# The third list of a routed expert layer goes through DRAM, with the low parts of one round's W2 on GpSimd and new urgencies for the searches

## The chip, the cores and the metric

One core of a Trainium2 chip runs the whole program. The metric is the device time of one execution in microseconds. Three executions of the kernel before took 650.06, 651.45 and 654.1 us, median 651.45. TensorE is the matrix engine (PE in the profile), VectorE is DVE, ScalarE is ACT, GpSimd is POOL; SyncE (SP) issues most transfers.

## The reference

```python
# q, k, v: 8 batches x 8 heads x 576 tokens x 64; heads 0-3: plain window of 32,
# heads 4-7: every 4th of the last 128 keys
attn = softmax(where(mask, q @ k.T / 8, -1e9)) @ v
x = attn, tokens as rows                         # 4608 x 512
logits = x @ w_gate                              # 8 experts
for idx in argsort(-logits.flatten()):           # best pair of token and expert first
    tok, e = idx // 8, idx % 8
    if assigned[tok] >= 0 or counts[e] >= 576: continue
    assigned[tok] = e; counts[e] += 1
out[assigned == e] = relu(x[assigned == e] @ w1[e]) @ w2[e]   # w1: 512 x 1024, w2: 1024 x 512
```

Each expert takes exactly 576 tokens. Inputs and result are float32.

## The kernel before

The first part computes the attention and the logits and writes the token rows to a DRAM tile `xd`; it ends near 200 us. The change does not touch it. The second part, `moe`, runs eight rounds, numbered 0 to 7 here. Round r serves the expert that fills up as the r-th, and its tokens are the r-th list (round 0 has the first list, round 2 the third).

A list is found by a search (`search`): eight steps, each a count on TensorE (`R.counts`, nine small matmuls, L841) and a chain of some ten small VectorE instructions (`R.step`, `R.remain`), one waiting for the other. Then `settle` finds the members, ranks them (L1118), closes the expert (`close`, `leave`, `start`: what the next search needs, and a copy of the choices on ScalarE, L982) and writes the list: `listing` makes flags on VectorE (`within`, L1176), a product on GpSimd and one on ScalarE, sums them on TensorE (`place`, L1195), and VectorE writes the indices (L1207).

`gather` fetches the 576 rows of x by five indirect transfers on GpSimd (four of 128 rows, one of 64). For the first rounds TensorE transposes each tile (L1396, four transposes into the one PSUM tile `ptx`). From round `QUARTERS` on it calls `spread` instead: the gathered tile goes to DRAM (L1420) and comes back in four pieces (L1424), arranged so that VectorE's transpose of 32x32 blocks (L1430) gives what is wanted, with the contraction rows in another order; W1 for these rounds comes from `in_moe_w1q`, which has the same order. Only two row tiles (`XG[5]`, `XG[6]`) serve the five gathers of `spread`; a gather waits until the store of the tile before the last is done.

Everything is multiplied in two parts: a high part rounded by ScalarE (`xh`, `w1h`, `w2h`, `hb`) and a low part, the difference (`xl`, `w1l`, `w2l`). The first product (L1460) takes, for each block of 128 hidden units, columns 0 to 255 of the list (its first two tiles) and columns 256 to 575 (the other three); the second (L1506 to L1511) takes one tile of tokens after the other. The low parts of the weights are VectorE subtractions (L1245), except those named in `ADDED`: there ScalarE writes the negated high part (L1271) and a GpSimd transfer adds the raw weight to it (L1273).

The order of the instructions on each engine is fixed when the program is built, by a list scheduler (`Schedule.run`). Each operation has a cost, dependences, perhaps an added latency `lat`, and a boost. Its due time is the end of the plan less the longest path behind it (its own cost included) less its boost. Of the operations that are ready on an engine the one due first is taken; others may fill a gap. Boosts are in nanoseconds: a larger one makes an operation more urgent. `B_C[r]` is the boost of the chain of search r and of closing its list, `B_L` that of the list itself, `B_G` that of gathers. On the chip every engine then works through its own order, waiting at each instruction for what it needs; a transfer waits in the same way on the queue of the engine that issues it.

Of the kernel before, what the change touches and what calls it, by code (L numbers as in the profile page):

```python
# [37 lines left out]
HI16, LO16 = -4128832, 4128831  # L38
HIGH = 65536.0
TOL_DVE, TOL_ACT, TOL_POOL, TOL_PE, T_W = 100, -50, 200, 500, 730  # L40
T_P, T_S, AHEAD = 310, 2200, 5
B_L, B_G, B_T, B_X, B_H, B_HL, B_Y, B_S, B_W = 23000, 27000, 15000, 0, 20000, 17000, 28000, -15000, 1500
RAW1, D_R, NQ, AHEAD_W = 8, 262, (2, 2), (3, 4)
QUARTERS, POOLED, T_B, T_H, B_R = 3, range(0), 5000, 2500, 20000
ADDED, T_A, T_G, T_L = (("2", 0), ("1", 1), ("2", 1)), 4500, 4500, 3500
T_D = {"1": 5000, "2": 4000}
NS, B_E, DIRECT, T_I = (2, 2), 3000, 7, 5000
B_C = (0, 2500, *(20000 + -16000 * (r >= QUARTERS) for r in range(2, 8)))
P_U, B_A, B_K, B_V, B_P, TOL_A, TOL_B, TOL_C, TOL_D = 4680, 15400, -5200, 14500, -105500, 650, 650, 300, 800
Q_ENG = (("POOL", "POOL", "POOL", "ACT"), ("DVE", "DVE", "ACT", "ACT"))  # L50
MSZ = (128, 128, 128, 128, 64)
# [119 lines left out]
class Schedule:  # L171
# [9 lines left out]
    def op(self, eng, cost, fn, deps=(), boost=0, lat=0, dma=0, buf=None, mode=64, tail=None):  # L181
        x = Op(len(self.ops), eng, cost, fn, deps, boost, lat, dma, buf)
        x.mode = mode
        x.tail = self.LAT if tail is None else tail
        for d in x.deps:
            d.users.append(x)
        self.ops.append(x)
        return x
# [1023 lines left out]
def moe(tc, ctx, C, R, xd, ROWS, w1, w1q, w2, out):  # L1212
# [8 lines left out]
    op = K.op  # L1221
# [24 lines left out]
    E, gemm1_end, x_users, got, gate = {}, {}, {}, {}, {}  # L1246

    def weights(n, r, f, deps):

        raw, old, use = RAW[n].take()  # L1250
        if n == "1" and r < len(AHEAD_W) and f == AHEAD_W[r]:

            gate[r] = op("POOL", 100, lambda: nc.gpsimd.memset(raw[:1, :1], 0.0), [got[r, 1], *old], B_G)
        if r in gate:
            deps = [*deps, gate[r]]

        def load():
            if n == "1":
                src = (w1 if r < QUARTERS else w1q)[bass.ds(E[r], 1), f].rearrange("o p d f -> p (o d f)")
            else:  # L1260
                src = w2[bass.ds(E[r], 1), f * 128:f * 128 + 128, :].rearrange("o p d -> p (o d)")
            nc.sync.dma_start(raw, src)

        ld = op("SP", 60, load, [*deps, *old], dma=T_W, lat=T_D[n] if r > 1 else T_L if n == "1" and r in gate and r else 0)
        h, oldh, useh = WH[n].take()
        l, oldl, usel = WL[n].take()
        first = n == "1" and r == 0
        hi = op("ACT", 525, lambda: act(h, raw), [ld, *oldh, st["rows"] if first else None], B_W)
        if (n, r) in ADDED:
            use.append(hi)  # L1270
            ne = op("ACT", 525, lambda: nc.scalar.activation(l, h.bitcast(F32), AF.Copy, scale=-1.0), [hi, *oldl], B_W)  # L1271
            useh.append(ne)
            lo = op("POOL", 1040, lambda: nc.gpsimd.dma_start(l, raw, accum_op=OP.add), [ne], B_W, lat=T_A)  # L1273
            use.append(lo)
        elif n == "2" and r >= 2 and f in POOLED:
            lo = op("POOL", 1350, lambda: sub(nc.gpsimd, l, raw, h), [ld, hi, *oldl], B_W)
            use += [hi, lo]
        else:
            lo = op("DVE", 600, lambda: sub(nc.vector, l, raw, h), [ld, hi, *oldl, st["list"] if first else None], B_W)
            use += [hi, lo]  # L1280
        useh.append(lo)
        return h, l, hi, lo, useh, usel


    def chain(eng, cost, fn, deps, boost=None):
        return op(eng, cost, fn, deps, B_C[len(scan)] if boost is None else boost)

    st, scan = {"place": None}, []

    def search(r):  # L1290
        scan.append(r)
        prev = st["next"]
        hold = gemm1_end.get(r - AHEAD) if r != 2 else gemm0[1]
        g = prev + [hold]
        for v in range(2):
            for it in range(4):
                early = 20000 if r == 1 and 4 * v + it < 1 else None
                p = chain("PE", T_P, R.counts, g if it == 0 else g[:1], early)

                def dve(v=v, it=it):  # L1300
                    R.step(it, v)
                    if it < 3:
                        R.remain(it, v)
                    if it == 3 and v == 0:
                        R.low(R.R, R.delta)
                        R.flags(R.V2, None, R.kstep(0, True))

                cost = T_S + (130, -330, -90, -1010 if v else 105)[it]
                g = [chain("DVE", cost, dve, [p, *g[1:]], early)]

        def which():
            R.count()
            R.fills()
            R.expert(R.largest())
            R.above()

        return chain("DVE", 2310, which, [g[0], st["fetch"]])

    def settle(r, e):

        if r == 0:
            m = rk = None
            nd = st["need"] = chain("DVE", 160, R.need_first, [], B_L)
        elif r < NE - 1:
            m = chain("DVE", 920, R.members, [e], B_L)
            rk = chain("PE", 70, R.ranks, [m], B_L)
            nd = st["need"] = chain("DVE", 270, R.need_of, [m, st.get("slots")], B_L)
        else:
            nd = chain("DVE", 400, R.rest, [e, st["left"], st["slots"]], B_L)
            rk = chain("PE", 70, R.ranks, [nd], B_L)  # L1330
        ac = chain("DVE", 1045, R.accept, [rk, nd], B_L)
        sl = st["slots"] = chain("DVE", 250, R.slots, [ac, st.get("digits")], B_L)
        ix, box = listing(r, sl)
        st["left"] = None
        if r == NE - 2:
            st["left"] = chain("DVE", 350, R.taken, [ac])
        elif r < NE - 1:
            cl = chain("DVE", 1930, R.close, [nd, ix if r == 0 else None])
            lv = chain("DVE", 830, R.leave, [cl, ac])
            gf = chain("DVE", 670, R.start, [cl])  # L1340
            st["next"] = [lv, gf]
        return ix, box

    def listing(r, sl):
        d = st["digits"] = op("DVE", 485, R.digits, [sl, st["place"]], B_L)
        t, old, use = PTR.take()
        lows, c1 = [], 0
        for n in OB[r > 0]:
            c0, c1 = c1, c1 + n
            lows.append((op("DVE", 110 + (36 if r == 0 else 26) * n, lambda c0=c0, c1=c1: R.within(c0, c1), [d], B_L), c0, c1))  # L1350
        halves = [(0, 14), (14, NCH)] if r == 0 else [(0, NCH)]
        xs = [(op("POOL", 150 + (30 if r == 0 else 18) * (c1 - c0), lambda c0=c0, c1=c1: R.by_chunk(c0, c1), [d], B_L),
               op("ACT", 250 + 9 * (c1 - c0), lambda c0=c0, c1=c1: R.by_row(c0, c1), [d], B_L)) for c0, c1 in halves]
        st["rows"] = xs[-1][1]
        prev = [*xs[0], *old]
        if r == 0:
            for (x, c0, c1), y in zip(lows, (xs[0], xs[1], xs[1])):
                prev = [op("PE", 27 * (c1 - c0), lambda c0=c0, c1=c1: R.place(t, c0, c1), [*prev, x, *y], B_L)]
        else:
            prev = [op("PE", 470, lambda: R.place(t, 0, NCH), [*prev, *(x[0] for x in lows)], B_L)]  # L1360
        st["place"] = prev[0]
        box = []
        ix = st["list"] = op("DVE", 780, lambda: box.append(R.indices(t)), prev, B_L)
        use.append(ix)
        return ix, box
# [71 lines left out]
    last, turns, gemm0, puts = [None], [], {}, {}  # L1437
# [110 lines left out]
    def round_(r):  # L1548
        e = None
        if r:  # L1550
            e = search(r) if r < NE - 1 else chain("DVE", 980, R.last, [st["fetch"], st["need"], st["left"]])
        en = st["fetch"] = EN[r] = op("SP", 100, lambda: fetch(r, R.eidx), [e])
        ix, BOX[r] = settle(r, e)
        X[r] = gather(r, ix, BOX[r])
        if r < NE - 2:
            lv, gf = st["next"]
            oc = (chain("ACT", 1055, lambda: R.copies(R.oh, nc.scalar), [lv]) if r else
                  chain("DVE", 640, lambda: R.copies(R.oh, nc.vector), [lv]))
            st["next"] = [oc, gf]
        W[r] = [weights("1", r, f, [en]) for f in range(NF)]  # L1560

    round_(0)
    for r in range(NE):
        W2 = [weights("2", r, f, [EN[r], X[r][-1][0] if r == 1 else None]) for f in range(NF)]
        expert(r, X[r], BOX[r], W[r], W2)
        if r + 1 < NE:
            round_(r + 1)
# [79 lines left out]
```

## Time and profile before

| | |
|---|---|
| median of three runs | 651.45 us (650.06 to 654.1) |
| profiled execution | 653.12 us, its span 651.4 us |
| TensorE busy | 618.2 us, 95% of the span |
| VectorE, ScalarE, GpSimd busy | 463.3, 304.4, 212.0 us |
| granted TensorE clock, mean | 0.975 |
| DMA | 110.97 MB, mean 170 GB/s |

The span is the time from the first to the last instruction; the rest of the profiled execution lies around it. Times in the rows below count from the span's start. Round 0's first product begins at about 206 us, round 1's at 264, round 2's at 325.5, and the rounds after it are 51 to 55 us long.

### The profile page before, as it was taken

To read this page: it belongs to the slowest core of one execution; us is meant where nothing else is said; L and a number is where in the kernel's file an instruction comes from. 1 tells how busy PE (TensorE), PEld (TensorE's weight loads), DVE (VectorE), ACT (ScalarE), POOL (GpSimd) and SP (SyncE) were. 2 spreads that over 40 slices of the span, in tenths; PEclk is the share of its full clock that TensorE was granted. 3 is DMA by queue.
4 is the path that set the end of the run, shared out by engine and by line. 5 is a ranking of instruction groups with operands and counts; after the bars stand their busy time and mean duration, and the time that the engine had idled before them with its cause. 6 is when DMAs were issued, how large, how long until landed. Compare 5 with 4: busy or idle time off the path is not lost.

```text
span 651.4 us, 18440 instructions
## 1 busy us (share of the span) xinstructions
PE 618.2 (95%) x7084; PEld 538.6 (83%) x7084; DVE 463.3 (71%) x1566; ACT 304.4 (47%) x675; POOL 212.0 (33%) x316
## 2 busy tenths in 40 slices
PE   7899899999858999999999999999999999999996
PEld 5788788879645988997799789789879979988985
DVE  4667577777678884799899999889889765624300
ACT  5676566666303825754445155235325425524211
POOL 6356467566004317333221221213112142011011
PEclk9899899999957999999999999999999999999999
DMA  8888898887206837997258338417716977302001
GB/s 240 228 245 238 236 261 253 218 244 203 80 3 191 222 82 195 284 189 253 76 157 273 107 109 268 156 62 254 212 41 211 272 229 234 107 34 73 1 25 48
DMA packets 68008, 110.97 MB, mean 170 GB/s; under 512 B 9168, under 2 KB 30544, under 8 KB 67920
## 3 DMA queue, kind: packets, MB, share of 16 engines
q1 hardware_dynamic: 58576, 84.62, 43.4%
q0 software_dynamic: 9344, 25.17, 14.5%
q8 instruction: 55, 0.90, 0.6%
q14 instruction: 33, 0.27, 0.1%
HBM read 78.69 MB, written 24.77 MB: 159 GB/s over the span
## 4 chain that ended last, share of the span: by engine, by line
PE 79%; DVE 8%; issue 5%; ACT 3%; DMA 2%; POOL 2%; SPq 0%; POOLq 0%; DVEq 0%; ACTq 0%
PE ph L1460 28%; PE py L1506 23%; PE px L550 4%; PE pS L538 4%; PE px L609 3%; PE py L1509 2%; PE py L1511 2%; PE pz L841 2%; PE pm L526 1%; PE pS L533 1%; PE pm L522 1%; PE pz L927 1%; DMA const<-in_cf 1%; POOL xg L1382 1%; PE ptx L1195 1%
## 5 line engine op out<-in xcount | busy, mean ns | idle before, releaser
L1506 PE MATMUL py<-w2h,hb 128*128 128x512 f32 x512 | 168.5, 396 | 0.0
L1460 PE MATMUL ph<-xh,w1h 128*128 128x256 f32 (+1 forms) x512 | 137.6, 299 | 0.8 <-ACT xh L1244 0.7
L1460 PE MATMUL ph<-xh,w1l 128*128 128x256 f32 (+1 forms) x512 | 136.2, 297 | 0.0
L1460 PE MATMUL ph<-xl,w1h 128*128 128x256 f32 (+1 forms) x512 | 136.2, 296 | 0.0
L1506 PEld LDWEIGHTS py<-w2h,hb 128*128 128x128 f32 x512 | 96.2, 188 | 18.9
L1244 ACT ACTIVATE hb<-ph 128x320 fp32r<-128x320 f32 (+2 forms) x192 | 59.8, 346 | 92.2 <-PE ph L1460 88.8
L1506 PE MATMUL py<-w2l,hb 128*128 128x512 f32 x256 | 99.8, 390 | 0.0
L1460 PEld LDWEIGHTS ph<-xh,w1h 128*128 128x128 f32 x512 | 91.9, 190 | 1.8 <-ACT xh L1244 0.9
L1460 PEld LDWEIGHTS ph<-xh,w1l 128*128 128x128 f32 x512 | 91.7, 190 | 0.1
L1460 PEld LDWEIGHTS ph<-xl,w1h 128*128 128x128 f32 x512 | 91.6, 190 | 0.0
L1532 POOL DMA_INDIRECT out<-y,idx x40 | 40.8, 1020 | 152.9 <-ACT y L1244 119.2
L1481 DVE SCALAR_TENSOR_TENSOR hb<-ph,hb 128x320 fp32r<-128x320 f32 (+1 forms) x128 | 57.0, 454 | 32.3 <-ACT hb L1244 29.5
L1244 ACT ACTIVATE y<-py 128x512 f32<-128x512 f32 (+1 forms) x40 | 23.9, 598 | 102.6 <-PE py L1506 91.3
L1414 POOL DMA_INDIRECT xg<-xd,idx x25 | 29.1, 1162 | 98.3 <-DMA rows<-xg 81.1
L492 ACT ACTIVATE E<-pS 128x384 f32<-128x384 f32 x96 | 44.9, 492 | 28.0 <-PE pS L538 27.3
L1506 PEld LDWEIGHTS py<-w2l,hb 128*128 128x128 f32 x256 | 48.2, 188 | 8.4
L550 PE MATMUL px<-v,E 128*64 128x65 f32 x1152 | 48.7, 224 | 5.0 <-issue 3.8
L538 PE MATMUL pS<-q,k 128*64 128x64 f32 x1152 | 53.0, 229 | 0.0
L550 PEld LDWEIGHTS px<-v,E 128*64 128x64 f32 x1152 | 42.4, 137 | 9.7 <-issue 5.8
L318 POOL COPY v<-v 32x520 f32<-32x520 f32 (+2 forms) x56 | 34.1, 633 | 49.1 <-DMA v<-in_vp 20.5
L538 PEld LDWEIGHTS pS<-q,k 128*64 128x64 f32 x1152 | 48.7, 144 | 0.0
L1245 DVE TENSOR_TENSOR w2l<-raw,w2h 128x512 fp32r<-128x512 f32 x48 | 31.7, 684 | 23.2 <-ACT w2h L1244 22.9
(217 smaller groups left out, 1123.6 us busy)
## 6 DMA issues: line engine op xcount, KB each, us to landing
raw<-in_moe_w SPq DMA_DIRECT2D x88, 256.0 KB
raw<-in_moe_w1q SPq DMA_DIRECT2D x40, 256.0 KB
rows<-xg SPq DMA_DIRECT2D x20, 256.0 KB
xg<-rows SPq DMA_DIRECT2D x80, 64.0 KB
qs<-in_qp SPq DMA_DIRECT2D x16, 288.0 KB
k<-in_kp SPq DMA_DIRECT2D x16, 288.0 KB
qs<-in_qd SPq DMA_DIRECT2D x16, 288.0 KB
k<-in_kd SPq DMA_DIRECT2D x16, 288.0 KB
```

Of the source, the lines that this page charges most:

```text
L318: f(t[:32, c0 + 1:c1 + 1], t[96:, c0:c1])
L492: e = self.op("ACT", 475, lambda j=j, pS=pS: nc.scalar.activation(self.E[:, 3 * j:3 * j + 3].rearrange("p c x -> p (c x)"), pS.tile[:, :38 ...
L538: x = nc.tensor.matmul(pS[64 * h:64 * h + 64, k, :, h], self.K[:, 32 * g:32 * g + 64], self.Q[:, g], start=False, stop=True, skip_group_ch ...
L550: x = nc.tensor.matmul(px[64 * h:64 * h + 64, c - c0, a], self.E[:, k, 64 * a:64 * a + 64], self.V[:, k, 2 * self.ui + a], start=True, sto ...
L609: x = nc.tensor.transpose(pt.tile[:, 128 * (c - c0):128 * (c - c0) + 128], xs[:, c, 2 * ui:2 * ui + 2].rearrange("p a d -> p (a d)"), C["i ...
L1244: act = lambda o, i, f=AF.Copy: nc.scalar.activation(o, i, f)
L1245: sub = lambda e, o, a, b: e.tensor_tensor(o, a, b, op=OP.subtract)
L1414: nc.gpsimd.indirect_dma_start(out=rows[:n], out_offset=None, in_=xd, in_offset=bass.IndirectOffsetOnAxis(ap=box[0][:n, m:m + 1], axis=0))
L1460: nc.tensor.matmul(o, a[:, d * 128:d * 128 + 128], b[:, d, c0:c1], start=((d, i) == pairs[0]), stop=((d, i) == pairs[-1]))
L1481: hl = op("DVE", 335 if j == 0 else 400, lambda: nc.vector.scalar_tensor_tensor(hb[:, CAP + c0:CAP + c1], o, 0.0, hb[:, c0:c1], op0=OP.max ...
L1506: nc.tensor.matmul(py, x, w, start=(f + i == 0), stop=(f == NF - 1 and i == 2))
L1532: s = nc.gpsimd.indirect_dma_start(out=out, out_offset=bass.IndirectOffsetOnAxis(ap=box[0][:n, m:m + 1], axis=0), in_=y[:n], in_offset=None)
```

## The change

- `QUARTERS` goes from 3 to 2: round 2's gather uses `spread`, and its W1 comes from `in_moe_w1q`.
- W2 of round 1 leaves `ADDED`: its eight low parts become GpSimd subtractions.
- In the planner, loads of round 1 get the latency of later rounds (W2 4000 ns, the first tiles of W1 5000 ns, instead of 0).
- The third list's search is no longer held until round 1's first product has begun.
- Boosts of the searches: the second list's falls from 2500 to -4000, the third's from 20000 to 10000, the fourth's rises from 4000 to 20000, those of the fifth to seventh from 4000 to 12000. The third list's flags (`within`) get 11000 instead of 23000. The cost of a count in the planner falls from 310 to 280 ns.

```diff
-T_P, T_S, AHEAD = 310, 2200, 5
-B_L, B_G, ... = 23000, 27000, ...
+T_P, T_S, AHEAD = 280, 2200, 5
+B_O, B_L, B_G, ... = 11000, 23000, 27000, ...
-QUARTERS, POOLED, T_B, T_H, B_R = 3, range(0), 5000, 2500, 20000
-ADDED, T_A, T_G, T_L = (("2", 0), ("1", 1), ("2", 1)), 4500, 4500, 3500
+QUARTERS, T_B, T_H, B_R = 2, 5000, 2500, 20000
+ADDED, T_A, T_G, T_L = (("2", 0), ("1", 1)), 4500, 4500, 3500
-B_C = (0, 2500, *(20000 + -16000 * (r >= QUARTERS) for r in range(2, 8)))
+B_C = (0, -4000, 10000, 20000, 12000, 12000, 12000, 4000)
...
-  ld = op("SP", ..., lat=T_D[n] if r > 1 else T_L if n == "1" and r in gate and r else 0)
+  ld = op("SP", ..., lat=T_D[n] if r > 1 else T_L if n == "1" and r in gate and r else T_D[n] if r else 0)
...
-        elif n == "2" and r >= 2 and f in POOLED:
+        elif (n, r) == ("2", 1):
             lo = op("POOL", 1350, lambda: sub(nc.gpsimd, l, raw, h), [ld, hi, *oldl], B_W)
...
-        hold = gemm1_end.get(r - AHEAD) if r != 2 else gemm0[1]
+        hold = gemm1_end.get(r - AHEAD)
...
-            lows.append((op("DVE", ..., lambda: R.within(c0, c1), [d], B_L), c0, c1))
+            lows.append((op("DVE", ..., lambda: R.within(c0, c1), [d], B_O if r == 2 else B_L), c0, c1))
```

## Rows read from the trace of the kernel before

**Rows 1.** Busy time by stretch: stretch, length, engines' busy us (instructions), PEclk, DMA share, GB/s.
```profile
265.40:325.70 60.30, 59.76 (x478) 52.03 (x478) 54.50 (x235) 33.86 (x73) 22.27 (x28) 1.00 0.70 188
325.70:380.60 54.90, 54.90 (x398) 48.23 (x396) 49.76 (x171) 22.38 (x51) 12.50 (x17) 1.00 0.51 164
...
250.90:264.60 13.70, 13.70 (x72) 10.97 (x70) 2.80 (x5) 5.20 (x9) 9.04 (x13) 1.00 0.85 238
264.60:293.50 28.90, 28.77 (x268) 28.01 (x267) 25.76 (x117) 19.92 (x47) 11.48 (x14) 1.00 0.96 222
```
**Rows 2.** All waits of TensorE, 211.3 to 646 us: total us, times, longest.
```profile
PE ptx L1396 <- DVE xl L1245: 0.2, 1, 0.2
PE pz L841 <- issue: 0.2, 1, 0.2
```
**Rows 3.** TensorE's timeline: start us, duration, line, operands, count.
```profile
313.01 0.60 PE L1396 MATMUL ptx<-const,xg 128*128 128x128 f32 x4
...
313.68 0.40 PE L1506 MATMUL py<-w2l,hb 128*128 128x512 f32 x1
313.92 0.63 PE L1506 MATMUL py<-w2h,hb 128*128 128x512 f32 x2
...
325.51 0.63 PE L1460 MATMUL ph<-xh,w1h 128*128 128x256 f32 x4
...
328.51 0.75 PE L1460 MATMUL ph<-xh,w1h 128*128 128x320 f32 x4
```
**Rows 4.** VectorE's groups over the span: count, busy us, mean ns, idle before.
```profile
L1481 DVE SCALAR_TENSOR_TENSOR hb<-ph,hb 128x320 fp32r<-128x320 f32 (+1 forms) x128 | 57.0, 454 | 32.3 <-ACT hb L1244 29.5 <-issue 1.3
...
L1430 DVE STREAM_TRANSPOSE xg<-xg 128x512 f32<-128x512 f32 (+1 forms) x25 | 15.9, 647 | 3.2 <-DMA xg<-rows 3.2
```
**Rows 5.** Low parts of W2, 262 to 300 us: ns min/median/max, first and last start.
```profile
L1273 POOL DMA_DIRECT2D w2l<-raw x8: 853/862/919, 271.5 to 285.9; - x8
```
**Rows 6.** GpSimd's timeline.
```profile
244.56 0.84 POOL L1181 TENSOR_TENSOR rx<-oa,const 128x360 bf16<-128x360 bf16 x1 [0.91 <-DVE oa L1176]
...
412.39 0.91 POOL L1414 DMA_INDIRECT xg<-xd,idx  x1 [10.13 <-DMA rows<-xg]
```
**Rows 7.** VectorE's timeline.
```profile
244.39 2.30 DVE L1176 TENSOR_TENSOR ob<-si,const 128x384 bf16<-128x384 int16 x6
...
248.94 0.33 DVE L1207 SCALAR_TENSOR_TENSOR idx<-t 64x5 int32<-64x5 f32 x2
...
298.11 1.79 DVE L1176 TENSOR_TENSOR ob<-si,const 128x384 bf16<-128x384 int16 x6
...
302.73 0.33 DVE L1207 SCALAR_TENSOR_TENSOR idx<-t 64x5 int32<-64x5 f32 x2
...
388.12 0.33 DVE L1207 SCALAR_TENSOR_TENSOR idx<-t 64x5 int32<-64x5 f32 x2
...
431.96 0.42 DVE L1245 TENSOR_TENSOR xl<-xg,xh 128x256 fp32r<-128x256 f32 x1
```
**Rows 8.** TensorE's timeline, counts, ranks and a first product.
```profile
206.31 0.44 PE L841 MATMUL pz<-G,ohr 128*128 128x64 bf16 x9
...
217.79 0.44 PE L841 MATMUL pz<-G,ohr 128*128 128x64 bf16 x9
...
242.19 0.21 PE L1118 MATMUL pz<-ge,const 128*128 128x72 bf16 x1
...
264.60 0.44 PE L841 MATMUL pz<-G,ohr 128*128 128x64 bf16 x9
...
268.13 0.82 PE L1460 MATMUL ph<-xh,w1h 128*128 128x320 f32 x4
...
291.28 0.21 PE L1118 MATMUL pz<-ge,const 128*128 128x72 bf16 x1
```
**Rows 9.** ScalarE's timeline.
```profile
250.30 1.16 ACT L982 ACTIVATE ohr<-oh 128x1152 bf16<-128x1152 bf16 x1 [0.74 <-DVE oh L960]
...
265.77 0.38 ACT L1244 ACTIVATE xh<-ptx 128x256 fp32r<-128x256 f32 x1
```

More of the change, by code (lines that the diff above doesn't have):

```diff
@@ L40 @@
 TOL_DVE, TOL_ACT, TOL_POOL, TOL_PE, T_W = 100, -50, 200, 500, 730
-T_P, T_S, AHEAD = 310, 2200, 5
-B_L, B_G, B_T, B_X, B_H, B_HL, B_Y, B_S, B_W = 23000, 27000, 15000, 0, 20000, 17000, 28000, -15000, 1500
+T_P, T_S, AHEAD = 280, 2200, 5
+B_O, B_L, B_G, B_T, B_X, B_H, B_HL, B_Y, B_S, B_W = 11000, 23000, 27000, 15000, 0, 20000, 17000, 28000, -15000, 1500
 RAW1, D_R, NQ, AHEAD_W = 8, 262, (2, 2), (3, 4)
-QUARTERS, POOLED, T_B, T_H, B_R = 3, range(0), 5000, 2500, 20000
-ADDED, T_A, T_G, T_L = (("2", 0), ("1", 1), ("2", 1)), 4500, 4500, 3500
+QUARTERS, T_B, T_H, B_R = 2, 5000, 2500, 20000
+ADDED, T_A, T_G, T_L = (("2", 0), ("1", 1)), 4500, 4500, 3500
 T_D = {"1": 5000, "2": 4000}
 NS, B_E, DIRECT, T_I = (2, 2), 3000, 7, 5000
-B_C = (0, 2500, *(20000 + -16000 * (r >= QUARTERS) for r in range(2, 8)))
+B_C = (0, -4000, 10000, 20000, 12000, 12000, 12000, 4000)
 P_U, B_A, B_K, B_V, B_P, TOL_A, TOL_B, TOL_C, TOL_D = 4680, 15400, -5200, 14500, -105500, 650, 650, 300, 800
@@ L1262, in load @@
             nc.sync.dma_start(raw, src)
-        ld = op("SP", 60, load, [*deps, *old], dma=T_W, lat=T_D[n] if r > 1 else T_L if n == "1" and r in gate and r else 0)
+        ld = op("SP", 60, load, [*deps, *old], dma=T_W, lat=T_D[n] if r > 1 else T_L if n == "1" and r in gate and r else T_D[n] if r else 0)
         h, oldh, useh = WH[n].take()
@@ L1349, in listing @@
             c0, c1 = c1, c1 + n
-            lows.append((op("DVE", 110 + (36 if r == 0 else 26) * n, lambda c0=c0, c1=c1: R.within(c0, c1), [d], B_L), c0, c1))
+            lows.append((op("DVE", 110 + (36 if r == 0 else 26) * n, lambda c0=c0, c1=c1: R.within(c0, c1), [d], B_O if r == 2 else B_L), c0, c1))
         halves = [(0, 14), (14, NCH)] if r == 0 else [(0, NCH)]
```

## The prediction, made before the result was known

> **What bounds the kernel now.** I read the page first, then the stretches of the expert part, then TensorE's waits, then the timelines of TensorE, VectorE and GpSimd around the third list. [...] Between 211.3 and 646 us it waits twice, 0.2 us each [rows 2]. So a microsecond of TensorE work taken out of rounds 0 to 2 is a microsecond of time, as long as the next operands are there. No other engine is at its bound for a whole round, but VectorE is close: 54.50 of 60.3 us in round 1, against 2.80 of 13.7 us just before the search for the third list [rows 1].
>
> **What the change takes from TensorE.** Five groups of transposes for the third list (four of 128 rows, one of 64) leave round 1's second product. One group starts at 313.01 and the second product behind it at 313.68; two neighbouring products without a group are 0.24 us apart (313.68 and the one behind it, 313.92), so a group costs 0.67 - 0.24 = 0.43 us [rows 3]. Five make 2.2 us, and with them goes the 0.22 us for which one group waited for the single PSUM tile [rows 2, 3]: 2.4 us. The upper bound is five whole durations of 0.60 us and the wait, 3.2 us; the lower, with the small group at half price and the wait staying, 2.0 us. I take 2.4, since it is measured in place.
>
> **What it adds.** VectorE gets the five transposes in blocks that each of the five later lists has, 25 in 15.9 us, so 3.2 us [rows 4]; its subtractions stay. They are hidden: the 13.7 us ahead of the search held 2.80 us of VectorE work [rows 1], and the search moves there. If that room were not used, VectorE would be at 57.7 of some 58 us in round 1 and the low parts of the hidden rows would come late, up to 3.2 us on TensorE. The five stores and twenty reads of the scratch trip go through SyncE, behind and before the weight loads; the trip's reads wait there for its store. Round 2 carries the same trip for the fourth list, with the same loads queued behind it, at 54.90 us of TensorE in 54.9, so I cost the queue at nothing [rows 1]; without that cover a load of W1 for round 2 would be late, by a wait of some us at 323. DMA had a share of 0.96 from 264.6 to 293.5 us [rows 1]: eight accumulating transfers of 256 KB leave just this stretch, and the trip (1.1 MB out, 1.1 MB back) falls mostly in the next.
>
> **W2 of round 1.** Eight ScalarE negations and eight GpSimd transfers (0.86 us to issue each, the last at 285.9 us) go [rows 5]; eight GpSimd subtractions of 128x512 f32 come. No such row exists. The nearest is a two-input GpSimd product, 128x360 bf16, at 0.84 us [rows 6]: by elements 1.2 us, twice that if the wider type counts in full. I take 1.2 us, by the same kind of operation. Eight are 10 us (up to 19), where GpSimd had 11.48 us busy of 28.9 [rows 1], seven of them in the transfers that go. The last high part and its negation were done when the last transfer was issued, at 285.9 us [rows 5], so the last low part is there near 287 to 288; the second product starts at 293.5. Cover about 5 us; if it goes, TensorE waits on the last low parts, and the list's gathers queue behind them on GpSimd. The later counting of weights (4 and 5 us in the planner instead of 0) only moves their loads ahead and their uses back; cost nothing, with the same cover.
>
> GpSimd's arithmetic also costs VectorE something. Six flag products of VectorE took 2.30 us with the GpSimd product lying on them and 1.79 us when it was nearly over: 0.51 us for 0.84 us [rows 6, 7]. Eight subtractions then cost VectorE 0.6 x 10 = 6 us if all lie on such operations, 0 if none does; I take a third, 2 us, as an estimate: most of a search step is small operations with one input. [...]
>
> **Is the third list in time?** This decides. Before, its indices are ready at 303.06 us and round 2's first product begins at 325.51, its second column block at 328.51 [rows 3, 7]. With 2.4 us less these become 323.1 and 326.1; the last low part of x is wanted 1.2 us later, at 327.3. A trip through the scratch, measured for the fifth list: indices at 388.45, the fifth tile's low part done at 432.38: 43.9 us, because only two row tiles serve five gathers (the fifth runs at 412.39, after 10.13 us of waiting for a store) [rows 6, 7]. So the indices are wanted by 327.3 - 43.9 = 283.4 us, 19.7 us sooner than before. What gives this, each an estimate from rows:
> - The hold goes: its first count ran at 264.60, just behind round 1's first product [rows 8]; its inputs are ready at about 251.5, when ScalarE has copied the choices [rows 9]. 13.1 us.
> - From ranks to indices the third list took 11.8 us (291.28 to 303.06), since closing the list and starting the next search came between; the second list took 7.1 (242.19 to 249.27) [rows 7, 8]. With the scratch path ahead of it, the list is now due sooner than the next search, even with its boost cut to 11000. 4.7 us.
> - In the empty 13.7 us a search step meets no low part of hidden rows, 0.45 us each [rows 4]. Four or so of the eight steps lie there: 1.7 us.
> - The second list's search loses 6500 of boost, but the planner counts backwards: by its own costs the two-tile trip lengthens the path from that search by some 13 us more than the old path through round 1, so it is due about 6 us sooner in all. Its second step ran 11.5 us after its first (206.31, 217.79) [rows 8], so there is room. 0 to 6 us.
> Sum 19.5 to 25.5, less 2 for GpSimd: 17.5 to 23.5, against 19.7. I forecast a wait between 0 and 2 us, likeliest none.
>
> **Sum.** 651.4 - 2.4 = 649.0 us of span. The profiled execution took 653.12 (span and 1.7 around it), 1.7 above the median; the same 2.4 on the median 651.45 gives 649.0.
>
> **Rivals.**
> 1. The list comes late (slower). Without the last item and with the list still behind the next search, the indices are at 303.06 - 13.1 - 1.7 = 288.3; the fifth tile is 5 us late, the wait falls ahead of round 2's second column block, and the time is 651.45 - 2.4 + 5 = 654; with the step to 293, which a full VectorE would give, 659. It is slower than before from a wait of 2.4 us, that is from indices later than 285.8. For it: the 43.9 us trip and the small margin. Against: the empty VectorE stretch. 22%, most of it 652 to 657.
> 2. [...] 9%.
> 3. The second list comes late, because its search is less urgent after all. Its last tile's high part was ready at 266.15, 2 us before its first use at 268.13 [rows 8, 9]; 6.5 us later gives a wait of up to 4.5: 649 + 4.5 = 653.5. Against: the longer path behind it. 6%.
> 4. The saving is taken up in small waits (SyncE, the changed order of counts): 651 to 652. 8%.
> 5. More than the transposes: fewer bubbles as the searches move into empty stretches; 645 to 647. 5%.
> The forecast, 647.5 to 651, has 50%.
>
> **Numbers.** Predicted 649.0. The range 646.2 to 656.5 takes in the forecast, rivals 2 to 4, the run scatter of before (650.06 to 654.1) and rival 1 up to a wait of 7.5 us. Faster by over 1% (below 644.9) would need 6.5 us, more than twice the upper bound of what leaves TensorE: 3%. Slower by over 1% (above 658, about what a measurement here tells from no change) needs a wait of 9 us, the far end of rival 1: 9%. Within 1%: 88%.
>
> **What would show it.** Right: round 1's stretch 2.4 us shorter with no transposes in it; the third list's first count near 252 us, indices near 280 to 284; TensorE's waits still under 2 us after 211; GpSimd subtractions of 1.2 to 2.4 us ending before 290. Wrong: a wait of TensorE for a high or low part of x near 326 us (rival 1); flag products of 2.3 us and more under GpSimd's subtractions and late indices (2); a wait near 264 us (3); second products of round 1 waiting for low parts of W2.

## The result and the profile after

The changed kernel took 660.61 us (median of six, 656.46 to 662.83) against 653.07 us for the kernel before beside it (six, 650.06 to 656.33): a ratio of 1.0113, interval 1.0067 to 1.0159. I had forecast 649.0 with a range to 656.5 and gave a loss of over 1% a chance of 9%. The profiled execution took 659.57 us, its span 657.8.

The part ahead of the experts begins the first product anywhere from 201.95 to 211.78 us in the profiles of this study, in code that the change leaves alone. So beside each ratio I use a second number, **the experts' part**: the span less the start of round 0's first product (L1460). TensorE's timeline of the kernel before has that start at

```profile
205.73 0.74 PE L1460 MATMUL ph<-xh,w1h 128*128 128x256 f32 x4 [0.69 <-ACT xh L1244]
```

which gives 651.4 - 205.73 = 445.7 us. Of the changed kernel, TensorE's timeline has that product, the third list's first count, and the instructions that waited longest (in brackets the wait and what ended it):

```profile
204.78 0.74 PE L1460 MATMUL ph<-xh,w1h 128*128 128x256 f32 x4 [0.69 <-ACT xh L1244]
...
250.25 0.44 PE L841 MATMUL pz<-G,ohr 128*128 128x64 bf16 x9
...
258.03 0.42 PE L841 MATMUL pz<-G,ohr 128*128 128x64 bf16 x9 [1.66 <-DVE G L1176]
...
282.16 0.22 PE L1118 MATMUL pz<-ge,const 128*128 128x72 bf16 x1 [2.24 <-DVE ge L1075]
...
288.54 0.24 PE L1195 MATMUL ptx<-rx,ob 128*128 128x40 bf16 x3 [0.90 <-DVE ob L1176]
...
298.10 0.43 PE L841 MATMUL pz<-G,ohr 128*128 128x64 bf16 x9 [1.25 <-ACT ohr L982]
```

The experts' part is 657.8 - 204.78 = 453.0 us, 7.3 longer. All waits of TensorE in the stretch of [rows 2], where there were 0.4 us:

```profile
PE pz L1118 <- DVE ge L1075: 2.2, 1, 2.2
PE pz L841 <- DVE G L1176: 2.1, 2, 1.7
PE pz L841 <- ACT ohr L982: 1.2, 1, 1.2
PE ptx L1195 <- DVE ob L1176: 0.9, 1, 0.9
PE ph L1460 <- ACT xh L1244: 0.5, 1, 0.5
PE ptx L1396 <- DVE xl L1245: 0.3, 1, 0.3
PE ph L1460 <- DVE hb L1481: 0.2, 1, 0.2
```

They sum to 7.4 us, 7.0 more than before. Busy time by stretch, as in [rows 1], with a short stretch behind the wait at 282:

```profile
265.40:325.70 60.30, 55.28 (x412) 48.65 (x410) 55.86 (x202) 25.30 (x56) 24.66 (x26) 0.97 0.65 196
325.70:380.60 54.90, 54.39 (x394) 47.73 (x393) 49.24 (x168) 24.50 (x55) 12.29 (x16) 1.00 0.53 162
250.90:264.60 13.70, 11.71 (x80) 8.89 (x78) 9.70 (x42) 6.96 (x13) 9.52 (x15) 1.00 0.92 235
...
282.00:286.00 4.00, 3.84 (x19) 3.84 (x18) 3.83 (x17) 2.02 (x4) 1.25 (x3) 0.57 0.90 309
```

TensorE was full in round 1 [rows 1] and now lacks 5 of 60.3 us. VectorE went up only from 54.50 to 55.86, so its share does not explain it; its single instructions do. VectorE's timeline, start and duration first:

```profile
278.38 1.07 DVE L1024 TENSOR_SCALAR gg<-R,delta 128x36 bf16<-128x36 f32 x1
279.36 1.32 DVE L1025 TENSOR_SCALAR gg<-R,delta 128x36 bf16<-128x36 f32 x1
...
281.41 0.69 DVE L1075 TENSOR_TENSOR ge<-te,gg 128x72 bf16<-128x72 f32 x1
...
284.94 4.35 DVE L1176 TENSOR_TENSOR ob<-si,const 128x384 bf16<-128x384 int16 x6
...
290.46 0.33 DVE L1207 SCALAR_TENSOR_TENSOR idx<-t 64x5 int32<-64x5 f32 x2
...
293.33 1.95 DVE L955 TENSOR_SCALAR V<-key 128x36 f32<-128x36 uint16 x1
...
300.74 1.26 DVE L867 TENSOR_SCALAR R<-V,delta 128x36 f32<-128x36 f32 x1
```

In the kernel before these took 0.22, 0.23, 0.23, 1.79 to 2.30 [rows 7], 0.18 and 0.24 us; from VectorE's timeline there, the two `gg` and `V`:

```profile
289.58 0.22 DVE L1024 TENSOR_SCALAR gg<-R,delta 128x36 bf16<-128x36 f32 x1
...
289.73 0.23 DVE L1025 TENSOR_SCALAR gg<-R,delta 128x36 bf16<-128x36 f32 x1
...
294.32 0.18 DVE L955 TENSOR_SCALAR V<-key 128x36 f32<-128x36 uint16 x1
```

Together they now take some 7.2 us more (0.85 + 1.09 + 0.46 + 2.05 + 1.77 + 1.02, with 2.30 for `ob`). GpSimd's subtractions lie under them, in its timeline:

```profile
278.11 3.90 POOL L1245 TENSOR_TENSOR w2l<-raw,w2h 128x512 fp32r<-128x512 f32 x3 [1.91 <-ACT w2h L1244]
...
285.52 2.75 POOL L1245 TENSOR_TENSOR w2l<-raw,w2h 128x512 fp32r<-128x512 f32 x2
...
293.94 1.30 POOL L1245 TENSOR_TENSOR w2l<-raw,w2h 128x512 fp32r<-128x512 f32 x1
```

The first two of the three subtractions at 278.11 end at 279.40 and 280.64, the two `gg` at 279.45 and 280.68. `V` ends at 295.28, the subtraction of 293.94 at 295.24; that hold began at 293.33, 0.6 us ahead of this subtraction, while GpSimd issued a gather (292.95 to 293.92). In runs 6, 12 and 18 below, where no subtraction follows the gather, `V` starts as far into its issue (0.36, 0.36 and 0.39 us; 0.38 here) and takes 0.18 us. Under a subtraction the reduction `te` kept its 0.45 us (280.93), the transpose of blocks `F` its 0.21 us (299.38), and in run 12 an `hb` (its input in PSUM) took 0.49 us at 274.69, against 0.48 at 282.29 here with GpSimd idle. So the held instructions do not run slower in proportion: the two `gg`, `V` and `R` end 0.04 to 0.05 us behind a subtraction and `ge` 0.09, so each of these was held until GpSimd's instruction was over. Not every instruction with its operands in SBUF is held: `pr` (two inputs, 128x288 bf16) kept its 0.30 us at 280.60, as the third subtraction began, and that one took 1.42 us against 1.29 and 1.28 of the two before.

### The profile page after: what moved, and what is told of

Its sections match the earlier page's. It is cut to its first block, busy times and chain, and to the rows that moved or that the text cites. A ratio compares the mean times of both kernels' runs of the same rounds, so it can differ in the third digit from the quotient of the medians.

```text
span 657.8 us, 18451 instructions
## 1 busy us (share of the span) xinstructions
PE 616.4 (94%) x7064; PEld 536.6 (82%) x7064; DVE 475.3 (72%) x1571; ACT 300.1 (46%) x667; POOL 215.0 (33%) x316
## 4 chain that ended last, share of the span: by engine, by line
PE 69%; DVE 10%; issue 10%; DMA 5%; ACT 3%; POOL 2%; SPq 1%; POOLq 0%; DVEq 0%; ACTq 0%
PE ph L1460 23%; PE py L1506 21%; PE px L550 4%; PE pS L538 4%; PE px L609 2%; PE pz L841 2%; DMA out<-y,idx 1%; PE pm L526 1%; PE pS L533 1%; DMA qs<-in_qd 1%; PE pm L522 1%; PE py L1509 1%; PE py L1511 1%; DVE ob L1176 1%; PE pz L927 1%
## 5 line engine op out<-in xcount | busy, mean ns | idle before, releaser
L1460 PE MATMUL ph<-xh,w1h 128*128 128x256 f32 (+1 forms) x512 | 138.3, 301 | 1.3 <-ACT xh L1244 1.2
L1460 PE MATMUL ph<-xh,w1l 128*128 128x256 f32 (+1 forms) x512 | 136.7, 298 | 0.0
L1460 PE MATMUL ph<-xl,w1h 128*128 128x256 f32 (+1 forms) x512 | 136.7, 298 | 0.0
L1460 PEld LDWEIGHTS ph<-xh,w1h 128*128 128x128 f32 x512 | 92.6, 191 | 2.5 <-ACT xh L1244 1.6
L1460 PEld LDWEIGHTS ph<-xh,w1l 128*128 128x128 f32 x512 | 92.2, 191 | 0.0
L1460 PEld LDWEIGHTS ph<-xl,w1h 128*128 128x128 f32 x512 | 92.2, 191 | 0.1
L1414 POOL DMA_INDIRECT xg<-xd,idx x30 | 33.3, 1112 | 99.9 <-DMA rows<-xg 85.3
L538 PEld LDWEIGHTS pS<-q,k 128*64 128x64 f32 x1152 | 47.3, 141 | 0.2 <-issue 0.2
```

The source lines that it names most:

```text
L538: x = nc.tensor.matmul(pS[64 * h:64 * h + 64, k, :, h], self.K[:, 32 * g:32 * g + 64], self.Q[:, g], start=False, stop=True, skip_group_ch ...
L1414: nc.gpsimd.indirect_dma_start(out=rows[:n], out_offset=None, in_=xd, in_offset=bass.IndirectOffsetOnAxis(ap=box[0][:n, m:m + 1], axis=0))
L1460: nc.tensor.matmul(o, a[:, d * 128:d * 128 + 128], b[:, d, c0:c1], start=((d, i) == pairs[0]), stop=((d, i) == pairs[-1]))
```

## The experiments

18 runs, each against the kernel before on its own chip. A ratio is that of the mean times. The kernel before had a median of 651.64 us beside runs 1 to 4, 652.54 beside 5 to 8, 655.64 beside 9 to 12, 656.65 beside 13 to 16 and 651.64 beside 17 and 18 (the last two groups were on one chip); the expectations in microseconds were stated against about 652, so where the kernel before was slower the ratios are compared. The experts' part is from one profile each; the kernel before has 445.7 us, the changed one 453.0.

| kernel | ratio (interval) | experts' part, us |
|---|---|---|
| the change | 1.0113 (1.0067 to 1.0159) | 453.0 |
| 1 subtractions on 16 columns | 1.0033 (1.0009 to 1.0057) | 446.1 |
| 2 transfers again, counted late | 1.0143 (1.0102 to 1.0184) | 456.3 |
| 3 before, with GpSimd's subtractions | 1.0099 (1.0066 to 1.0132) | 452.8 |
| 4 subtractions in four pieces | 1.0114 (1.0082 to 1.0146) | 449.8 |
| 5 as 3, with pauses | 1.0094 (1.0061 to 1.0127) | 450.7 |
| 6 the lists alone | 1.0108 (1.0076 to 1.0141) | 449.8 |
| 7 VectorE subtracts | 1.0139 (1.0107 to 1.0171) | 455.7 |
| 8 the change with pauses | 1.0103 (1.0065 to 1.0142) | 451.6 |
| 9 as 6, seven raw buffers | 1.0039 (1.0008 to 1.0070) | 450.5 |
| 10 four transfers, four GpSimd | 1.0029 (1.0004 to 1.0054) | 448.6 |
| 11 six transfers, two GpSimd | 1.0050 (1.0027 to 1.0073) | 452.6 |
| 12 W1, W2 counted as before | 0.9991 (0.9968 to 1.0015) | 449.3 |
| 13 the change again | 1.0095 (1.0057 to 1.0134) | 453.1 |
| 14 only W2 counted later | 1.0043 (1.0016 to 1.0071) | 450.9 |
| 15 as 12, 16 columns | 0.9924 (0.9893 to 0.9954) | 444.8 |
| 16 as 12, five GpSimd, three transfers | 1.0016 (0.9991 to 1.0042) | 448.2 |
| 17 as 12, six GpSimd, two VectorE | 1.0069 (1.0039 to 1.0099) | 448.7 |
| 18 as 12, four GpSimd, four VectorE | 1.0024 (0.9996 to 1.0051) | 446.0 |

The two columns differ by up to 0.6% of the time for one kernel (runs 12 and 15). One profile stands beside six to twelve executions; whether that explains it is not shown. I rely on what both say.

**1. GpSimd nearly free.** From the changed kernel, order of every engine the same:

```diff
-lambda: sub(nc.gpsimd, l, raw, h)
+lambda: sub(nc.gpsimd, l[:, :16], raw[:, :16], h[:, :16])
```

> The changed kernel with every engine's order kept, but GpSimd's eight subtractions cover only 16 of 512 columns (the rest of W2's low parts of round 1 is left out). Theory A (GpSimd's arithmetic holds up VectorE instructions of the third list, and TensorE waits for them): the flags gg, V and ob fall back to 0.22, 0.18 and 1.8 to 2.3 us, TensorE's waits at ranks (2.2), place (0.9) and the count behind the choices (1.25) go, and the time is 653 to 656, 4 to 7 below the changed kernel's 660.6. Theory B (the search moved ahead, with its counts waiting in TensorE's order, and the scratch trip cost the time): those waits are not VectorE's slow instructions, and the time stays at 659 to 661.

Measured 654.31 us; `gg` back at 0.22 us, the waits at ranks and places gone. 453.0 - 446.1 = 6.9 us of the experts' part is GpSimd's work; by the ratios it is 1.0113 - 1.0033 = 0.8%, 5.2 us. What is left of TensorE's waits is 3.0 us, most of it this line:

```profile
PE ph L1460 <- ACT xh L1244: 2.1, 2, 1.6
```

The 1.6 us lie behind ScalarE's copy of `y`, which waited 3.57 us for its buffer, to 271.13; the output transfer that holds it had queued behind accumulating transfers of W1 (four issued from 257.24 on, the next outputs from 261.20; an output took 8.5 us in the median to land).

**2. The transfers back, W2 still counted late.**

```diff
-ADDED = (("2", 0), ("1", 1))
+ADDED = (("2", 0), ("1", 1), ("2", 1))
```

> The changed kernel with W2 of round 1 back among the negations and accumulating transfers, all else changed. Theory A: 651 to 655, no VectorE instruction held up in 275 to 305 us. Theory B: 658 to 661. If the list's trip is also too long for its place, a wait of 2 to 3 us for x near 326 us stays and the time is 653 to 655.

Measured 662.21 us, more than either theory allowed (651 to 655 and 658 to 661). No VectorE instruction is held, but one wait takes its place in TensorE's timeline:

```profile
312.78 0.80 PE L1506 MATMUL py<-w2l,hb 128*128 128x512 f32 x1 [6.53 <-DMA w2l<-raw]
```

It waits for the last accumulating transfer, which is issued only at 305.13 us, behind two gathers of the third list in GpSimd's queue (302.37 and 304.14); the first of these had waited 6.97 us for a store of the scratch trip.

**3. GpSimd's subtractions put into the kernel before**, and nothing else.

```diff
-ADDED = (("2", 0), ("1", 1), ("2", 1))
+ADDED = (("2", 0), ("1", 1))
...
-        elif n == "2" and r >= 2 and f in POOLED:
+        elif (n, r) == ("2", 1):
```

> The kernel before with one part of the change alone: W2's low parts of round 1 are GpSimd subtractions. Theory A: VectorE is held up in the third list's search, 655 to 660, 2 to 7 above before. Theory B: 652 to 654, no difference.

Measured 658.69 us, most of the change's loss. Here the hold is at its longest: VectorE's, GpSimd's and TensorE's timelines, and the clock of the stretch behind.

```profile
270.85 6.49 DVE L877 TENSOR_SCALAR e<-R,delta 128x72 int16<-128x72 f32 x1
```
```profile
269.74 7.53 POOL L1245 TENSOR_TENSOR w2l<-raw,w2h 128x512 fp32r<-128x512 f32 x6
```
```profile
277.88 0.64 PE L841 MATMUL pz<-G,ohr 128*128 128x64 bf16 x9 [5.86 <-DVE G L1176]
```
```profile
278.00:282.00 4.00, 4.00 (x26) 4.00 (x25) 2.83 (x11) 0.29 (x1) 0.00 (x0) 0.59 0.00 0
```

One instruction of 0.26 us waited for six subtractions without a gap between them, to 277.34; GpSimd's run ends at 277.27. The next count on TensorE is in its order ahead of products whose operands are there, so TensorE stood 5.86 us, and behind that its granted clock was at 0.59 for 4 us.

**4. The same subtractions in pieces of 128 columns**, in the changed kernel.

```diff
-lambda: sub(nc.gpsimd, l, raw, h)
+lambda: [sub(nc.gpsimd, l[:, c:c+128], raw[:, c:c+128], h[:, c:c+128]) for c in range(0, 512, 128)]
```

> The changed kernel with the same order, each GpSimd subtraction cut into four of 128 columns. If a VectorE instruction that meets GpSimd waits until the GpSimd instruction is over (theory A in its strict form), none is held longer than one short piece, some 0.3 to 0.4 us, gg falls from 1.1 and 1.3 to about 0.6, and the time is 655 to 658. If the two share the way to memory by turns, only the total of GpSimd work counts, the slow instructions stay as slow, and the time stays at 659 to 662. Theory B: 659 to 661 as well, whatever the instructions do.

Measured 659.08 us, as the change, and outside what the strict form of the theory forecast (655 to 658). Most holds did get shorter: a piece takes 0.45 to 0.6 us, the two `gg` take 0.23 and 0.51 us, and five of the `ob` 0.60 or 0.61 us each, about one piece. `V` alone is still held long, over the end of a gather's issue (287.90 to 288.88) and three pieces behind it. VectorE's timeline:

```profile
281.50 0.61 DVE L1176 TENSOR_TENSOR ob<-si,const 128x384 bf16<-128x384 int16 x1
...
288.28 1.95 DVE L955 TENSOR_SCALAR V<-key 128x36 f32<-128x36 uint16 x1
```

TensorE's waits in this profile are 4.4 us instead of 7.4. But the profiled execution (653.52 us) was the fastest of the seven, and the median did not move; why the time does not follow the holds stays open.

**5. Pauses.** Run 3 with GpSimd's pipeline drained ahead of each subtraction.

```diff
+nc.gpsimd.drain()
 sub(nc.gpsimd, l, raw, h)
```

> The kernel before with the six-back-to-back GpSimd subtractions of the third experiment (658.69 us there), and ahead of each of them GpSimd's pipeline is drained, so that there is a gap between two. Theory A (VectorE's instruction is kept out as long as GpSimd's two-input operations follow each other without a gap, and gets in at the first gap): the longest hold of a VectorE instruction falls from 6.49 us to about 1.4 us, one subtraction, TensorE's single 5.86 us wait splits or vanishes, and the time comes to 653 to 656 us. Theory B (VectorE is kept out for all of GpSimd's work, gap or not): the hold stays near 6.5 us and the time near 658 to 660 us.

Measured 658.06 us: theory A has the hold right (VectorE's longest is 1.26 us, and ends with one subtraction) and the time wrong. Two `TENSOR_SCALAR` are still held for 1 us (1.26 us at 277.80 and 1.25 at 285.57, instead of 0.24), and the subtractions, begun at 275.97, give W2's raw buffers back late: ScalarE waits 5.24 us for a raw weight with the copies of `hb` queued behind it, and TensorE 4.36 us. Why the `e` of run 3 did not get in between two subtractions without a gap, where the `gg` of the change did, stays open.

**6. The lists alone.** From the changed kernel:

```diff
+ADDED = (("2", 0), ("1", 1), ("2", 1))
...
+  ld = op("SP", ..., lat=T_D[n] if r > 1 else T_L if n == "1" and r in gate and r else 0)
```

> The changed kernel without two of its parts: the low parts of W2 of the second round are made by the accumulating transfer again, and W2 (and W1) of that round is counted in the order where it was before. What is left of the change is the third list by two row tiles and the second list's search made less urgent. Theory A (GpSimd's subtractions cost the changed kernel 6 to 7 us, the later count of W2 cost the second experiment its 6.5 us TensorE wait, and the lists' part saves the 2.4 us of transposes): no VectorE instruction is held, TensorE's wait for W2's low parts is under 1 us, and the time is 648.5 to 651.5 us against 651.6 us before. Rival (the lists' part itself loses what it saves, in waits of the third list's path): 652 to 656 us. Rival (the transfers of W2 are late with the earlier count too, since they stand behind the third list's gathers in GpSimd's queue): a wait of 4 us or more on W2 remains, 656 to 662 us.

Measured 660.24 us; the third expectation came out, the first failed. ScalarE's and TensorE's timelines, then the stretch 280 to 300 us of this kernel and of the kernel before:

```profile
291.60 0.63 ACT L1244 ACTIVATE w2h<-raw 128x512 fp32r<-128x512 f32 x1 [4.32 <-DMA raw<-in_moe_w]
```
```profile
294.57 0.42 PE L841 MATMUL pz<-G,ohr 128*128 128x64 bf16 x9 [4.07 <-DVE G L853]
```
```profile
280.00:300.00 20.00, 15.51 (x129) 14.79 (x128) 13.30 (x46) 11.29 (x26) 9.21 (x10) 0.91 1.06 302
```
```profile
280.00:300.00 20.00, 19.87 (x156) 18.07 (x153) 18.68 (x82) 10.04 (x23) 5.34 (x8) 1.00 0.94 240
```

The raw weight that ScalarE waits for is late for two reasons that the profile shows. SyncE's queue stood 13.4 us, to 276.55, for the number of the third list's expert (L1543), then issued eight loads of W1 for round 2, and only then this load. In the kernel before, the last two loads of W2 are issued at 275.66 and 277.08, ahead of its wait for that number; here, in SyncE's waits and its queue's timeline:

```profile
SPq L1543 <- DVE pr L1071: 13.4, 1, 13.4
```
```profile
277.31 5.49 SPq L1262 DMA_DIRECT2D raw<-in_moe_w1q  x8
283.06 8.26 SPq L1262 DMA_DIRECT2D raw<-in_moe_w  x5
```

The load, first of the five, then took 8.5 us to land (4.4 in the median), while the DMAs, with the list's gathers beside the accumulating transfers, were at a share of 1.06. `hb` and the next choices stand behind ScalarE's wait, VectorE waits for `hb`, and TensorE for the count. The third expectation has the time right, but the wait is at a count and not at W2. A kernel with those loads ahead of the expert's number was not run, so it is not shown that the low parts of W2 had to leave the DMAs for the list to come earlier.

**7. VectorE subtracts**, from the changed kernel.

```diff
-        elif (n, r) == ("2", 1):
+        elif False:
```

> The changed kernel with the low parts of W2 of the second round subtracted by VectorE in place of GpSimd: eight operations of about 0.68 us, 5.4 us of VectorE. Theory A (what the changed kernel loses is that GpSimd holds VectorE up, more than the 10.7 us of work itself): gg and V stay at 0.22 and 0.18 us, and the time is 651 to 655 us, near the 654.3 us with the subtractions cut to 16 columns. Rival (VectorE is full on the third list's path, so 5.4 us more of it costs what GpSimd's hold costs): ranks and places wait as in the changed kernel, and the time is 657 to 661 us.

Measured 661.95 us: the rival. No subtraction holds anything, but counts wait for VectorE one after the other (5.6 of 7.3 us of waits), and the clock falls:

```profile
300.00:315.00 15.00, 10.82 (x61) 7.37 (x58) 13.47 (x55) 0.91 (x2) 2.22 (x3) 0.66 0.63 178
```

**8. The change with pauses** (the edit of run 5).

> The changed kernel with GpSimd drained ahead of each of its eight subtractions. Theory A (a VectorE instruction gets in at each gap between two GpSimd operations): held instructions are held for at most one subtraction, about 1.4 us, of which the changed kernel has five to seven already; the time falls by 0 to 2 us, to 658 to 660.6 us. Theory B (holds depend on GpSimd's total work alone): 660 to 662 us, V and ob held as before.

Measured 659.99 us: a gain of at most 1 us, within A; no remedy.

**9. Seven raw buffers for W2, seven for W1**, in run 6.

```diff
-RAW1 = 8;  ("2", 6)
+RAW1 = 7;  ("2", 7)
```

> The kernel of the lists alone (sixth experiment, 660.24 us) with seven raw buffers for W2 in place of six, and seven for W1 in place of eight. Theory A (its 4.07 us TensorE wait came because a raw buffer of W2 was given back late by an accumulating transfer, so that ScalarE stood 4.32 us at w2h with hb behind it): SP's waits for w2l<-raw fall from 9.1 us to under 5 us, TensorE's wait to under 1.5 us, and the time is 649.5 to 654 us. Rival (the transfers themselves are slow, DMA share 1.05 to 1.08 from 280 to 300 us): a wait of 3 us or more for raw stays on ScalarE, and the time is 656 to 661 us.

Measured 657.63 us. By ratio, 1.0039, it lies between the two theories. ScalarE's wait for the raw weight is 3.3 us instead of 4.3, TensorE's 3.0. SyncE's waits for the accumulating transfers did not fall (9.7 us, 9.1 in run 6), and the last load of W2 is still issued behind seven of W1.

**10 and 11. Shares.** In run 6, GpSimd subtracts only from the fifth (run 11: the seventh) tile on.

```diff
-        if (n, r) in ADDED:
+        if (n, r) in ADDED and ((n, r) != ("2", 1) or f < 4):
```

> The kernel of the lists alone, with the last four of the eight low parts of W2 of the second round subtracted by GpSimd and the first four made by the accumulating transfer, W2 counted where the kernel before has it. Theory A (GpSimd's cost goes by its work, 10.7 us of it costing 6 to 7 us, and the transfers' cost comes when all eight share the DMAs with the third list's gathers): half of each, 653 to 657 us, holds of one or two VectorE instructions of at most 1.4 us each. Rival (either one is enough to make a wait of 4 us): 657 to 662 us.

> As the run before it, with six of the eight low parts by the accumulating transfer and the last two by GpSimd. Theory A (cost by GpSimd's work, and two transfers fewer are enough for the raw buffers to come free in time): 651 to 655 us, at most one held VectorE instruction on TensorE's path. Rival (the transfers' wait stays): a TensorE wait of 3 us or more behind w2h, 656 to 661 us.

Half and half came to 1.0029, in A's range, but with more holds than A allowed: the six `ob` take 4.04 us in all, `V` 2.01, and `A` and `Mo` 0.95 and 1.22 instead of 0.19 and 0.20. Six and two came to 1.0050 (659.44 us), on the edge of A's range and below the rival's; the wait of 7.4 us behind ScalarE's raw weight is the rival's, and the experts' part is longer than with eight transfers.

**12. W1 and W2 of round 1 counted where the kernel before has them**, GpSimd's subtractions kept.

```diff
-  ld = op("SP", ..., lat=... else T_D[n] if r else 0)
+  ld = op("SP", ..., lat=... else 0)
```

> The changed kernel with one part undone: W1 and W2 of the second round are counted in the order where the kernel before has them, GpSimd's eight subtractions stay. Theory A (the later count is not what costs; GpSimd's holds are): 659 to 662 us, VectorE instructions held again. Rival (the later count puts the subtractions beside the third list's ranks and places, and earlier ones would fall on less urgent work): 652 to 657 us.

Measured 655.21 us, level with the kernel before; the rival. The subtractions run from 270.9 to 286.6 us instead of 278.1 to 302, and waits of 3.3 us are left at ranks and places:

```profile
PE pz L1118 <- DVE ge L1075: 1.9, 1, 1.9
PE ptx L1195 <- DVE ob L1176: 1.4, 2, 1.1
```

**13 to 16, on one chip.** The change again; W2 alone counted later; run 12 with subtractions on 16 columns; run 12 with the last three low parts by the transfer.

```diff
# 14
+  lat=... else T_D[n] if r and n == "2" else 0)
# 16
-ADDED = (("2", 0), ("1", 1))
+ADDED = (("2", 0), ("1", 1), ("2", 1))
...
+        if (n, r) in ADDED and ((n, r) != ("2", 1) or f >= 5):
```

> The changed kernel as it is, beside the three others on one chip. Theory A (the later count of W2 puts GpSimd's subtractions where they hold up the third list's ranks and places and the fourth list's start): ratio to the kernel before 1.009 to 1.014 here too, the earlier count having been worth 1.2%. Rival (the chip of the run with the earlier count was another, and the gain was the chip's): under 1.005.

> The changed kernel with W1 of the second round counted where the kernel before has it, W2 alone later; TensorE's order is that of the changed kernel. Theory A (W2's later count is what costs): ratio 1.008 to 1.014. Rival (W1's count costs, since its accumulating transfers make y wait for its put): 0.997 to 1.004.

> The kernel with W1 and W2 counted back (0.9991) with GpSimd's eight subtractions on 16 of 512 columns, so that most of W2's low parts of the second round is left out and GpSimd is nearly free. Theory A (GpSimd's holds still cost 3 to 4 us there: the waits for ge 1.9 us and ob 1.4 us): ratio 0.992 to 0.997, no wait for ge or ob. Rival (there the holds fall on work that is not needed soon): 0.997 to 1.002.

> W1 and W2 counted back, GpSimd for the first five low parts of W2 of the second round and the accumulating transfer for the last three. Theory A (GpSimd is done by 278 us, ahead of gg and ob, and three transfers are not late): ratio 0.992 to 0.998, no wait for ge or ob over 0.5 us. Rival (w2h waits for a raw buffer that a transfer holds, as with six transfers and two subtractions): 1.002 to 1.008.

The change came out at 1.0095 again, with the same experts' part to 0.1 us, so the loss is not a chip's. 14, at 1.0043, lies between 12 and 13, just above its rival's range and well below A's: W1's later count costs too, by a mechanism that is not shown. The wait of 1.66 us at 258 is absent in 14, but also in runs 1, 2, 4, 7 and 8, which count W1 later as well, so W1's count alone does not make it. 15 leaves most of W2's low parts out, so it is a floor and no complete kernel: with GpSimd nearly free the rest of the change is a gain. TensorE's timeline has its first product, and of its waits there this is the longest:

```profile
211.78 0.74 PE L1460 MATMUL ph<-xh,w1h 128*128 128x256 f32 x4 [0.69 <-issue]
```
```profile
PE pz L841 <- DVE G L853: 0.9, 1, 0.9
```

Its profiled execution took 658.35 us against its median of 651.57, and nearly all of that excess lies ahead of the experts.

16 is level with the kernel before (1.0016, between its two theories): `gg`, `ob` and `V` are each held by one subtraction still (1.06, 3.27, 2.01 us), since the fourth and fifth run at 283.63 and 290.15 us and not before 278.

**17 and 18, run 12 with the last two, or four, low parts by VectorE.**

```diff
-        elif (n, r) == ("2", 1):
+        elif (n, r) == ("2", 1) and f < 6:
```

> W1 and W2 counted back, GpSimd for the first six low parts of W2 of the second round and VectorE for the last two. Theory A (the last two hold ob by 2.1 us, and VectorE has 1.4 us for them): ob at 2.2 us, no wait of TensorE for ob, ratio 0.993 to 0.998. Rival (VectorE's 1.4 us come ahead of G or the places and are waited for all the same): 0.998 to 1.004.

> The same with GpSimd for the first four and VectorE for the last four. Theory A (GpSimd is done before gg, VectorE's 2.7 us are spread): ratio 0.992 to 0.999. Rival (VectorE is full on the lists' path, as with all eight on it, 1.0139): 1.001 to 1.008.

17, at 1.0069, is above both its expectations: `ob` is free (2.19 us, no wait), but TensorE still waits 1.9 us for `ge`, which GpSimd holds, and 0.8 us for `xh`. 18 came to 1.0024, in its rival's range: TensorE's wait for `ge` is 0.2 us, its longest is 1.6 us at a count, the experts' part is 446.0 us, 0.3 from the kernel before, and the ratio's interval holds 1. No complete version beat the kernel before; runs 12, 16 and 18 equal it.

## Why the prediction was wrong

**The sum of the parts.** By the experts' part, taking the change apart from run 15 up: the lists and all that moved with them, 444.8 - 445.7 = -0.9 us; GpSimd's work in the earlier order 449.3 - 444.8 = 4.5; W2's later count 450.9 - 449.3 = 1.6; W1's 453.1 - 450.9 = 2.2; together 7.4. They are not independent: with GpSimd free first, both counts cost 446.1 - 444.8 = 1.3 and GpSimd 6.9. The ratios on one chip say the same in order (1.0095, 1.0043, 0.9924), with sizes up to 4 us apart; GpSimd's work is 4.4 to 5.2 us by the ratios of runs 12 and 15, and of run 1 and the change. Why run 15's ratio is 5 us below 1 while its experts' part is only 0.9 us shorter stays open.

**The step that failed: "I take a third, 2 us".** The forecast gave GpSimd's contention 2 us of VectorE and took them from the third list's slack of 17.5 to 23.5 us. Both halves were wrong. The size: 4.5 to 6.9 us of time, and some 7.2 us on VectorE, above even the upper bound of 6. I read [rows 6, 7] as a rate (0.51 us per 0.84 us of GpSimd) and held small instructions with one input to be safe. They show a hold. Taken one by one, five of the six flag products of [rows 7] took 0.35 us in the kernel before, and one this, in VectorE's timeline:

```profile
244.65 0.96 DVE L1176 TENSOR_TENSOR ob<-si,const 128x384 bf16<-128x384 int16 x1
```

It ended at 245.61, 0.21 us behind the end of GpSimd's product at 245.40. In the change `gg` (1.07 and 1.32 us), `V` (1.95) and `R` (1.26), which read one tile, were held too. The place: a list that is due later has slack in the plan, but TensorE's order is fixed, and ranks, places and the next search's counts stand between products. A hold there was a wait at once, whatever the list's due time: 2.24 us at the ranks, 0.90 at a place. The sign that the prediction marks (2) came, 4.35 us for six flag products and indices at 290.79, yet TensorE waited only 0.5 us for the list.

**"The later counting ... cost nothing" failed too**, by 1.6 + 2.2 = 3.8 us with the subtractions in it. It did not move all loads ahead: the last two of W2 went from 275.66 and 277.08 us (272.22 and 274.14 in run 12) to 284.11 and 284.68, behind SyncE's wait for the number of the third list's expert. The subtractions went with them, from 270.9 to 286.6 us (run 12) to 278.1 to 302, onto ranks, places and the fourth list's start. The same wait in SyncE's queue delayed W2 in run 6, so costing that queue at nothing was wrong as well.

**The third list.** First count at 250.25 (forecast 252): right. Indices at 290.79, not 280 to 284; the trip took 45.8 us (fifth tile's low part at 336.60) against 43.9 from [rows 6, 7]. They were wanted by 283.4, so rival 1 would have cost its full price; TensorE waited 0.5 us, since round 2 itself began at 332.66. That was luck: the other waits had put round 2 off already. In run 15 the list waited 0.3 us, so the search was moved by enough.

**The transposes** left TensorE as said: in the experts' part it is busy 437.60 us in run 15 and 439.75 in the kernel before, 2.15 us less with 20 transposes fewer. Run 15's waits take most of it back, 2.1 us where the kernel before has 0.4, so rival 4 is true as well; the experts' part got 0.9 us shorter.

**GpSimd's subtraction**: a median of 1.34 us, in the forecast's 1.2 to 2.4; the last ended at 302, not before 290, since it waited for ScalarE's high parts (3.67 us ahead of the last two, at 298.91).

**The clock** was at 0.57 for 4 us behind the wait at 282: 0.50 from 282.2 to 285.4 us, where neighbouring products of 128x320 are 0.27 us apart, and 1.00 from 285.6, where they are 0.15 apart. That accounts for an estimated (1 - 0.57) x 4 = 1.7 us. With 7.0 us of new waits and 2.4 us of transposes less that makes 6.3 of the 7.3 us; 1 us stays open, and it lies in TensorE's busy time, which is 440.17 us against run 15's 437.60 with only 1.7 of that from the clock. The second profile of it (run 13) has 1.00 in the whole stretch and other waits instead, with the same experts' part.

## What to carry to other kernels

Price work moved to GpSimd by the instructions of VectorE that it may hold: here the held ones ended with one subtraction (`gg`, 1.07 and 1.32 us instead of 0.22 and 0.23) or with a run of six (`e`, 6.49 instead of 0.26), and where TensorE's next instruction waited for one it stood 2.24 and 5.86 us. Slack in a due time is no slack on an engine whose order is written out: look for what stands next in that order. Before moving a job off a queue or an engine, try it on each of the others alone; here transfers lost behind a weight load late in SyncE's queue, VectorE by its own load and GpSimd by its holds, and with the later count undone runs 12, 16 and 18 came level. Look as well at what a load stands behind in its queue: moving a list moved it here.

## What the hardware showed that I had not expected

- One VectorE `TENSOR_SCALAR` of 0.26 us took 6.49 us, over six GpSimd subtractions without a gap; in the changed kernel two in a row were held by one subtraction each. What lets VectorE in between two is not shown.
- Cutting GpSimd's instruction in four shortened most holds (single `ob` of 0.60 us instead of 1.42 to 1.44), but not that of `V` (1.95 us); draining it in between left 1.26 us at most in run 5. Neither shortened the time (1.0114 against 1.0113, 1.0094 against 1.0099).
- A GpSimd subtraction of 128x512 f32 takes 1.28 to 1.80 us; VectorE's takes 0.68 (`w1l` at 297.83): a factor of two by the median of 1.34.
- Behind waits of TensorE of 2.24 us (the change) and 5.86 us (run 3) the granted clock of the next 4 us was 0.57 and 0.59. In the change it read 0.50 for an estimated (1 - 0.57) / 0.50 x 4 = 3.4 of the 4 us; at the same 0.50 run 3 has an estimated 3.3. Shorter waits went both ways: behind 1.91 us in run 17 it was 0.57 over 4 us, behind 1.92 us in run 12 and 1.78 us in run 13 it stayed at 1.00.
